# The first batch rebuilt: attention by token quarters, expert 0 alone on the first quarter, the other experts in seven-product chunks

## The chip, the cores and the metric

One core of a Trainium2 chip. The metric is the device time of one execution in microseconds (us), as a median over runs. PE is the matmul engine, DVE VectorE, ACT ScalarE, POOL GpSimd, SP the engine that issues the other DMAs. SBUF and PSUM are the two on-chip memories that the kernel's tiles lie in; PE's results come in PSUM. The granted clock is the share of PE's full clock that the profile shows as granted. L672 is line 672 of the kernel that the line of the profile comes from; a line inserted or removed shifts the numbers by a few from one kernel to the next.

## The reference, cut to what matters

```python
# attention: 4 batches, 8 heads, 768 tokens of 64, in 8 blocks of 96 tokens
P = sort_net                                   # 8x8 per head
for _ in range(5):                             # Sinkhorn: exp, rows, columns
    P = exp(P - P.max(-1)); P /= P.sum(-1) + 1e-9; P /= P.sum(-2) + 1e-9
k_sorted, v_sorted = P @ k_blocks, P @ v_blocks  # blocks mixed
x = softmax(q @ k_sorted.T / 8) @ v_sorted       # inside each block
# experts: x is (3072, 512), 4 experts of 512 -> 1024 -> 512
p = domain_probs / (domain_probs.sum(-1) + 1e-9)
out = sum(p[:, e] * (relu(x @ w1[e]) @ w2[e]) for e in range(4))
```

A batch is 768 rows of x. The work on PE is the experts' two layers; a batch's attention is made beside the experts of the batch before, except for batch 0, which has nothing before it.

## The kernel before: the parts that matter here

Batches 1 to 3 go in chunks of 256 tokens. Their second layer is not eight block products but seven (a Strassen-like scheme): sums of blocks of w2, made once (`weight_sums`), and sums of blocks of the hidden layer, made for each chunk (`h_sums`). Batch 0 goes by halves, an expert at a time, in the plain form, so it doesn't need the sums. A slot is a place after a group of the experts' matmuls where stages of attention are put. Three tiles come up again: `vo` holds mixed v on its way to memory, `pb` holds the token weights of a chunk, and `natq` a batch's queries.

```python
def load_queries(b):                         # 8 loads, f32 to f16, so all on POOL's queue
    for h in range(H):
        nc.gpsimd.dma_start(t[:, h // 2, :, h % 2, :], q[b, h]...)

def weight_sums(e):                          # once for each expert, 128x1024 each
    tt = nc.gpsimd.tensor_tensor
    tt(t3, b22, b12, ALU.subtract)           # b11.. are the blocks of w2sb[e]
    tt(b12, b12, b11, ALU.subtract)
    tt(t2, b22, b12, ALU.subtract)
    tt(n4, b21, t2, ALU.subtract)

def chunk(b, c, slot):
    for e in range(E):
        for g in range(2):                   # first layer, Relu and token weight on DVE, h_sums
            ...
    # p1 uses w2's block b11; p4 is the second product and the first that uses a sum, n4
    nc.scalar.copy(p1[:], product("p1", blk(0, 0), "b11"))
    nc.scalar.copy(ob1, product("p4", blk(1, 1), "n4"))
    ...                                      # five more products
# ... (cut)
for qd in range(2):
    for nm in ("k", "v"):
        load_natural(1, nm, qd)
load_queries(1)
for e in range(2, E):                        # weights of experts 2 and 3 after batch 1's inputs
    load_w1(e); load_w2(e)
run(halves([(0, 0, 0), (0, 1, 0)]), ...)     # batch 0: halves of 384 tokens, expert by expert
# ... (cut)
run(halves([(0, 1, 1)]) + plain(lambda: weight_sums(0), lambda: weight_sums(1))
    + halves([(0, 2, 0), (0, 2, 1), (0, 3, 0)]) + plain(lambda: weight_sums(2)) + halves([(0, 3, 1)]),
    5 * SLOTS, attention_order(1))
builds(2)
weight_sums(3)                               # first needed in batch 1
for b in range(1, B):
    for c in range(R // 2):
        chunk(b, c, slot)
```

The softmax here doesn't subtract the row's maximum and nothing guards it: scores larger than these inputs give would overflow.

Of the kernel before, what the change touches and what calls it, by code (L numbers as in the profile page):

```python
# [9 lines left out]
F32 = mybir.dt.float32  # L10
# [7 lines left out]
def kernel(  # L18
# [105 lines left out]
    make_identity(nc, ident)  # L124
    load_natural(0, "v", 0)
    load_natural(0, "k", 1)
    load_natural(0, "v", 1)
    load_natural(0, "q", 1, 0, P // 2)
    for qd in range(2):
        load_natural(0, "q", qd, P // 2, P // 2)  # L130
# [10 lines left out]
    )  # L141

# [11 lines left out]
    kTs, ETs, vos, vs0s = [], [], [], []  # L154
# [12 lines left out]
    load_w1(0)  # L167
    load_w2(0)
    load_w1(1)
    load_w2(1)  # L170
    identf = Tt[2].rearrange("p a f x -> p (a f x)")[:, 0:2 * P].bitcast(F32)
    nc.gpsimd.tensor_copy(identf, ident[:])
# [4 lines left out]
    for n in range(1):  # L177
        vo = const.tile([P, R, 4, VW], F16, name=f"vo_{n}")
        nc.gpsimd.memset(vo[:, :, :, ds(D, 2)], 1.0)
        vos.append(vo)  # L180

    p_sb = const.tile([P, R, E], F32, name="p_sb")

    for r2 in range(2):
        for hf in range(2):
            nc.sync.dma_start(
                p_sb[ds(64 * r2, 64), ds(3 * hf, 3), :],
                moe_domain_probs[ds(hf * HS, HS)].rearrange("(p r s) e -> p r s e", r=3, s=2)[:, :, r2, :],
            )
# [10 lines left out]
    def q_half(b, pr, hf, copy):  # L200

        ps = psa([P, R, 64], F16, f"ps_q_{b}_{pr}_{hf}")
        for r in range(R):
            for hh in range(2):
                nc.tensor.transpose(
                    ps[ds(D * hh, D), r, :],
                    head(b, "q", 2 * pr + hh)[ds(64 * hf, 64), r, :],
                    ident[ds(64 * hf, 64), ds(64 * hf, 64)],
                )
        if (b, pr) not in qTs:  # L210
            qTs[(b, pr)] = from_spare(S).rearrange("p (i x) -> p i x", i=NB)
        copy(
            qTs[(b, pr)][:, ds(HB * hf, HB), :].rearrange("p i (r c) -> p i r c", r=R),
            ps.rearrange("p r (i c) -> p i r c", c=CP),
        )
# [3 lines left out]
    scol = const.tile([GH, NB, 1], F32, name="scol")  # L219
    for it in range(5):  # L220
        nc.scalar.activation(sn[:], sn[:], AF.Exp, bias=0.0, scale=1.0)
        nc.vector.tensor_reduce(srow[:], sn[:], AX.X, ALU.add)
# [9 lines left out]
    warm(28)  # L232
    for pr in range(2):
        q_half(0, pr, 0, nc.scalar.copy)
    warm(48)
# [49 lines left out]
    r_half(1)  # L285

# [3 lines left out]

    def evac(b):
        return nc.vector.tensor_copy if b == 1 else nc.scalar.copy

    def st_v(b, pr):
# [9 lines left out]
        vo = vos[0]  # L304
        evac(b)(
# [23 lines left out]
    def st_k(b, pr):  # L329
# [11 lines left out]
        evac(b)(  # L341
# [57 lines left out]
    xT0a = moe.tile([P, 2, R, NKC, 64], F16, name="xT0", tag="xT")  # L399
    xT0 = [xT0a[:, hf] for hf in range(2)]  # L400
    xsl0 = {}
    vT0 = {qd: from_spare(S) for qd in range(2)}

# [18 lines left out]
    def h_k(qd, hf):  # L422
        mix_half("k", qd, hf, kTs[qd][:, 0:S], nc.vector.tensor_copy)

    def h_v(qd, hf):
        mix_half("v", qd, hf, vT0[qd], nc.scalar.copy)

    def h_w(qd, hf):
        ps = psa([BLK, 2 * HB, P], F16, f"ps_w_{qd}_{hf}")
        vT = vT0[qd]  # L430
        for n in range(2 * HB):
            nc.tensor.transpose(ps[:, n, :], vT[:, ds(n * BLK, BLK)], ident[:])
        nc.vector.tensor_copy(
            vs0s[qd][:, :, :, :, 0:D].rearrange("c i s h d -> c (i s h) d"),
            ps.rearrange("c n (h d) -> c (n h) d", h=2),
        )
# [377 lines left out]
```

## Time and profile before

| kernel before | value | from |
|---|---|---|
| time | 392.28 us, median of 3 (391.88 to 393.17) | the runs |
| span of the profiled run | 390.3 us | first line of the page |
| PE, DVE, ACT, POOL busy | 95%, 59%, 21%, 27% of the span | the page, part 1 |
| first expert matmul / batch 1 begins | 28.64 / 134.20 us | timeline of PE |
| idle of PE in batch 0's stretch | 105.80 - 101.06 = 4.7 us | the stretches, shown in the prediction |

A busy share of 95% doesn't say where the other 5% lies. The stretches do: from batch 1 on PE is busy for 86.50 of 86.70 us, and the change leaves those batches as they are, so what it can shorten lies before, and the argument below is about when batch 1 begins. "Batch 1 begins" is the first first-layer matmul of batch 1's first chunk in PE's timeline. What follows it takes 256.1 us before (390.3 - 134.20). The prediction cut 0.2 us later, at 134.40.

### The profile page before, as it was taken

The numbers are of one execution on the slowest core, as the hardware profiler recorded it, in microseconds if no ns is written. First come the engines' busy times: TensorE is split into PE (matmuls) and PEld (weight loads), VectorE is DVE, ScalarE is ACT, GpSimd is POOL, SyncE is SP. The second block draws the span as 40 slices with busy tenths as digits, with TensorE's granted clock in tenths as the row PEclk, the third lists the DMA queues.
The fourth block names the chain that finished last, engine by engine and source line by source line (L and its number), as shares of the span: only waits on it lengthen the run. The fifth ranks groups of instructions, "written<-read, shape, count | busy, mean of one in ns | idle before, by whom it ended". The sixth has DMA issues, their size and how long they took to land.

```text
span 390.3 us, 8513 instructions
## 1 busy us (share of the span) xinstructions
PE 370.9 (95%) x3725; PEld 293.0 (75%) x3725; DVE 230.7 (59%) x413; ACT 81.7 (21%) x124; POOL 105.2 (27%) x125
## 2 busy tenths in 40 slices
PE   5678989989999999999999999999999999999995
PEld 5564555545555588888889888888889888888885
DVE  5452443353245288478578477488488485694773
ACT  2344242214433233201110032211110001000000
POOL 8452460029619980200390100100100100001001
PEclk9958999999999999999999999999999999999999
DMA  9999899977429949925194335313202101100101
GB/s 118 195 209 206 119 168 193 220 129 151 70 52 150 153 115 156 193 59 95 44 121 74 90 95 147 97 21 69 54 29 76 55 0 55 55 30 29 53 2 54
DMA packets 70822, 39.07 MB, mean 100 GB/s; under 512 B 42489, under 2 KB 65089, under 8 KB 70785
## 3 DMA queue, kind: packets, MB, share of 16 engines
q0 software_dynamic: 34624, 17.83, 36.0%
q1 hardware_dynamic: 36161, 20.70, 22.5%
q8 instruction: 29, 0.48, 0.5%
q14 instruction: 8, 0.07, 0.1%
HBM read 42.86 MB, written 8.76 MB: 132 GB/s over the span
## 4 chain that ended last, share of the span: by engine, by line
PE 88%; DMA 4%; DVE 4%; ACT 1%; POOL 1%; issue 1%; DVEq 0%; SPq 0%; ACTq 0%; POOLq 0%
PE ps_h L641 33%; PE ps_p L668 28%; PE ps_h L553 10%; PE ps_o L567 9%; DMA T<-in_q_dram 3%; DMA vs_dram<-vo 2%; PE ps_a L383 1%; DVE xsl L368 1%; PE ps_s L351 1%; PE ps_k L334 1%; PE ps_v L298 1%; PE ps_x L477 1%; ACT ET L451 1%; PE ps_s L444 1%; DVE kT L417 0%
## 5 line engine op out<-in xcount | busy, mean ns | idle before, releaser
L641 PE MATMUL ps_h<-xT,w 128*128 128x256 f16 x1152 | 130.3, 273 | 0.0
L641 PEld LDWEIGHTS <-w 128*128 128x128 f16 x1152 | 111.9, 98 | 14.9
L647 DVE SCALAR_TENSOR_TENSOR Hb<-ps_h,pb 128x1024 f16<-128x1024 f32 x72 | 88.1, 1223 | 30.6 <-PE ps_h L641 29.0
L668 PEld LDWEIGHTS <-Sb 128*128 128x128 f16 x576 | 55.8, 98 | 7.5 <-issue 0.7
L688 POOL TENSOR_TENSOR oa<-u,p 128x256 f32<-128x256 f32 x9 | 6.5, 723 | 182.7 <-issue 164.7
L553 PE MATMUL ps_h<-xT,w 128*128 128x384 f16 x256 | 46.7, 332 | 0.2 <-ACT xT L480 0.2
L668 PEld LDWEIGHTS <-Hb 128*128 128x128 f16 x432 | 41.8, 98 | 4.8
L567 PE MATMUL ps_o<-w,Hb 128*128 128x512 f16 x192 | 43.8, 379 | 0.0
L553 PEld LDWEIGHTS <-w 128*128 128x128 f16 x256 | 24.3, 99 | 16.6 <-issue 1.5
L559 ACT ACTIVATE Hb<-ps_h 128x768 f16<-128x768 f32 x32 | 25.9, 811 | 48.4 <-PE ps_h L553 48.4
L668 PE MATMUL ps_p<-w,Sb 128*128 128x256 f16 x288 | 34.4, 273 | 0.4 <-DVE u L687 0.4
L668 PE MATMUL ps_p<-w,Hb 128*128 128x256 f16 x288 | 34.4, 273 | 0.0
L668 PE MATMUL ps_p<-T,Sb 128*128 128x256 f16 x288 | 33.6, 273 | 0.0
L567 PEld LDWEIGHTS <-Hb 128*128 128x128 f16 x192 | 18.1, 98 | 20.2 <-ACT Hb L559 0.5
L358 ACT ACTIVATE ET<-ps_s 96x768 f16<-96x768 f32 x24 | 18.0, 802 | 44.5 <-PE ps_s L351 44.5
L578 DVE SCALAR_TENSOR_TENSOR oacc<-ps_o,p_sb,oacc 128x512 f32<-128x512 f32 x18 | 13.5, 749 | 17.1 <-PE ps_o L567 17.1
L681 ACT COPY p<-ps_p 128x256 f32<-128x256 f32 x9 | 3.4, 373 | 93.0 <-PE ps_p L668 74.8
L368 DVE TENSOR_TENSOR xsl<-ps_a,rz 96x512 f16<-96x512 f32 x32 | 22.0, 687 | 1.1
L103 POOL DMA_DIRECT2D natq<-in_q_dram x24 | 19.8, 862 | 0.0
L93 POOL DMA_DIRECT2D nat_k<-in_k_dram x8 | 6.3, 787 | 42.9 <-PE ps_k L334 33.1
L668 PE MATMUL ps_p<-T,Hb 128*128 128x256 f16 x144 | 17.2, 273 | 0.0
L93 POOL DMA_DIRECT2D nat_v<-in_v_dram x8 | 6.1, 761 | 37.9 <-PE ps_v L298 31.5
(98 smaller groups left out, 321.8 us busy)
## 6 DMA issues: line engine op xcount, KB each, us to landing
w<-in_moe_w_dram POOLq DMA_DIRECT2D x8, 1024.0 KB, 18.2
pb<-p_dram SPq DMA_DIRECT2D x9, 512.0 KB, 4.4
nat_k<-in_k_dram POOLq DMA_DIRECT2D x8, 384.0 KB, 5.5
nat_v<-in_v_dram POOLq DMA_DIRECT2D x8, 384.0 KB, 7.1
vs_dram<-vo SPq DMA_DIRECT2D x6, 396.0 KB, 4.6
vs<-vs_dram SPq DMA_DIRECT2D x6, 396.0 KB, 3.7
natq<-in_q_dram POOLq DMA_DIRECT2D x24, 96.0 KB, 4.7
out_dram<-ob SPq DMA_DIRECT2D x9, 256.0 KB, 2.0
```

The source lines that it names most:

```text
L93: nc.gpsimd.dma_start(t[ds(p0, pn)].rearrange("p h r d -> p h (r d)"), src[b, ds(4 * qd, 4)].rearrange("h (p r) d -> p h (r d)", r=R)[ds(p ...
L103: nc.gpsimd.dma_start(t[:, h // 2, :, h % 2, :], q[b, h].rearrange("(t p) d -> p t d", p=P))
L358: nc.scalar.activation(ETs[2 * (pr % 2) + hh][:, 0:S].rearrange("c (a x) -> c a x", a=2), pss[hh][0:BLK, :, 0:HS], AF.Exp, bias=0.0, scale ...
L368: nc.vector.tensor_tensor(xsl[:, :, hh, :].rearrange("c (a i) d -> c a i d", a=2), av[:, :, :, 0:D], rz[:].broadcast_to([BLK, 2, HB, D]), ...
L553: nc.tensor.matmul(ps[:, a, 0:HS], w1sb[e][:, kc, ds((2 * f2 + a) * P, P)], xT0[hf][:, :, kc, :], start=(kc == 0), stop=(kc == NKC - 1),)
L559: nc.scalar.activation(hT[:, ds(2 * f2, 2), :], ps[:, :, 0:HS], AF.Relu, bias=0.0, scale=1.0,)
L567: nc.tensor.matmul(ps[:], hT[:, fc, ds(t * P, P)], w2sb[e][:, fc, :], start=(fc == 0), stop=(fc == NFC - 1),)
L578: nc.vector.scalar_tensor_tensor(out=oaccs[(b, col)][:], in0=ps[:], scalar=pcol, op0=ALU.mult, in1=oaccs[(b, col)][:], op1=ALU.add,)
L641: nc.tensor.matmul(ps[:, f, :], w1sb[e][:, kc, ds((4 * g + f) * P, P)], xT[:, kc, ds(2 * c * P, 2 * P)], start=(kc == 0), stop=(kc == NKC ...
L647: nc.vector.scalar_tensor_tensor(out=Hb[:, e, ds(4 * g, 4), :], in0=ps[:], scalar=0.0, op0=ALU.max, in1=pb[:, ds(e, 1), :].broadcast_to([P ...
L668: nc.tensor.matmul(ps[:], lhs(e, f), Ts[e][rhs][:, f, :], start=(e == 0 and f == 0), stop=(e == E - 1 and f == KH - 1),)
L688: nc.gpsimd.tensor_tensor(oa2, u2[:], p5[:], ALU.add)
```

## The change

Its intent: batch 0 gets the cheaper seven-product form for experts 1 to 3, and starts earlier, since expert 0 can begin as soon as the first quarter (192 tokens) of attention is done. The price is that the sums of w2 are needed in batch 0, so POOL makes them early, and the weights are loaded before batch 1's inputs. The diff, cut to its core:

```diff
+    load_w1(0); load_w2(0); (two query loads); load_w1(1); load_w2(1)   # among the first loads
+    for e in range(2, E):
+        load_w1(e)
+        load_w2(e)
 # ... h_q: one transpose group and one copy for a head quad's queries
+        copy(
+            qT0[qd][:, :, ds(HS * hf, HS)].rearrange("p s (x r) -> p s r x", r=R),
+            ps[:],
+        )
 # ... the token weights of all batches normalized at the start, on 24 partitions
+    def spread_weights():
+        normalized(p_out.rearrange("t e p -> t p e"), p_in, p_den)
+        nc.sync.dma_start(p_dram.rearrange("e (t p) -> t e p", p=P), p_out)
+        pbs[(0, 0)] = load_p(0, 0)
 # ... second layer of experts 1 to 3 in batch 0
-            for e in range(E):
+            for e in es:                         # 1 to 3 in batch 0
 # ... the order of the main program
     builds(1)
+    weight_sums(1)
     for qd in range(2):
         for nm in ("k", "v"):
             load_natural(1, nm, qd)
     load_queries(1)
-    for e in range(2, E):
-        load_w1(e); load_w2(e)
-    run(halves([(0, 0, 0), (0, 1, 0)]), 2 * SLOTS, second, 2)
-    ...
+    first_layer0(0, next_stages)
+    first_layer0(1, next_stages)
+    second_layer0(0, next_stages)
+    weight_sums(2)
+    chunk_first(0, 0, [1], 1, next_stages)
+    weight_sums(3)
+    first_layer0(2, no_stages)
+    h_x(3, vec)
+    first_layer0(3, no_stages)
+    second_layer0(1, no_stages)
-    for b in range(1, B):
+    for b in range(B):
+        plan = PLAN if b else PLAN0
```

## The prediction

> **What bounds the kernel now.** I read the page first, then the stretches of the span, then the timeline of PE, the chain of waits, and the timelines of POOL and of the DMA issues. Stretches first (the columns are busy us of each engine, granted PE clock, DMA share, GB/s); I cut the span where PE's timeline shows the first expert matmul, then the first matmul of each later batch:
>
> ```profile
> 0.00:28.60 28.60, 18.29 (x324) 16.65 (x325) 14.90 (x49) 10.13 (x18) 17.86 (x43) 0.81 1.19 173
> 28.60:134.40 105.80, 101.06 (x879) 55.30 (x877) 41.20 (x71) 36.70 (x47) 50.20 (x43) 0.99 1.02 147
> 134.40:221.10 86.70, 86.50 (x906) 75.36 (x905) 61.51 (x103) 15.77 (x25) 28.31 (x28) 1.00 0.62 102
> 221.10:307.80 86.70, 86.50 (x907) 75.49 (x905) 59.48 (x103) 15.76 (x25) 4.49 (x6) 1.00 0.29 75
> 307.80:390.30 82.50, 78.56 (x720) 70.16 (x718) 53.66 (x88) 3.35 (x9) 4.36 (x6) 1.00 0.11 40
> ```
>
> From 134.4 us on PE has no gap worth naming (86.50 of 86.70): batches 1 to 3 are matmul-bound and the change leaves them alone. All that can move is the first 134.4 us. It holds 28.6 us of opening and 105.8 us for batch 0, 19 us more than a later batch takes. The last matmuls of the opening and PE's later gaps (bracket: idle before, and what ended it):
>
> ```profile
> 28.02 0.82 PE L477 MATMUL ps_x<-ident,xsl 96*128 96x96 f16 x8 [1.42 <-DVE xsl L368]
> 28.64 0.84 PE L553 MATMUL ps_h<-xT,w 128*128 128x384 f16 x2
> 29.73 2.03 PE L553 MATMUL ps_h<-xT,w 128*128 128x384 f16 x6 [0.25 <-ACT xT L480]
> ...
> 39.13 0.50 PE L444 MATMUL ps_s<-Sb,kT 64*128 64x96 f16 x15 [0.91 <-DVE kT L417]
> ...
> 53.83 0.50 PE L477 MATMUL ps_x<-ident,xsl 96*128 96x96 f16 x8 [1.15 <-ACT ET L451]
> ...
> 88.08 0.50 PE L351 MATMUL ps_s<-qT,kT 64*128 64x96 f16 x15 [1.32 <-DVE vo L305]
> ```
>
> In the chain, warm groups of batch 0 take 1.30 us for 8 first-layer matmuls of 384 columns (2.60 for 16) and 1.73 us for 8 second-layer matmuls of 512 (3.46 for 16). There are 32 and 24 such groups: 41.6 + 41.5 = 83.1 us. Attention stages lying between them, at the starts in the chain (0.46 to 0.50 us each, 0.30 for queries), are about 6.8 us for the second half of batch 0 and 7.0 us for batch 1. The other 9 us of the stretch are gaps (some 4.7 us, listed in part above), the half clock at its start, and about 0.1 us at each change of stage.
>
> **What the Trainium skill says.** "TensorE: Matmul & The Clock Gate", section "Back-to-back issue gap", gives N/2.4 + 2.5 ns warm for N columns. The trace agrees: 16 matmuls of 256 columns take 1.75 us, 109 ns each (formula 109.2). I use its 82.5 ns for the new 192-column matmuls, which the trace of before doesn't have; that is an estimate. The same page, Part 1, says that the clock is halved after an idle window of about 3.4 us and restored after a busy one. The trace grants 0.50 from 18 to about 30 us, and full clock some 2 us after the dense expert matmuls begin, so the sparse opening runs at half clock. "DMA: Bandwidth & Descriptors", section "SWDGE vs HWDGE vs iDMA", says that a cast during a transfer is possible only on GpSimd's queue. So every f32 to f16 load here is one queue and costs POOL time to issue: below, 6.57 us for one batch's queries. "GPSIMD Engine Reference", section "Key points", says POOL shares SBUF interfaces with VectorE; here POOL's weight sums last 2.12 to 2.21 us beside busy and idle VectorE alike, so I add nothing for it.
>
> **Part by part.** (1) Fewer products. Experts 1 to 3 change from 18 second-layer groups (18 x 1.73 = 31.1 us) to three chunks of seven products of 12 matmuls, 252 x 109 ns = 27.5 us. Their first layers are 3 x 6 groups of 16, 18 x 1.75 = 31.5 us, against 24 x 1.30 = 31.2. Expert 0's first layer is 128 x 82.5 ns = 10.6 us against 10.4; its second is unchanged. Sum: 83.1 becomes 80.0, 3.1 us less on the path, as PE is the bound there.
>
> (2) An earlier start. The first quarter needs one score group and one attend group per head quad instead of whole halves. I walked the new opening with the trace's durations (PE at half clock: transposes of a head quad 0.8 us, ACT copies and exponentials 0.75 to 0.8, kT copies 0.96, normalizing 0.2 + 0.69). Sinkhorn ends at 11.3 as now; queries transposed within it cost PE 0.6 us ahead of ps_R; k copied at 15.9, v at 18.0; the new normalizing of all token weights on 24 partitions is an estimated 2.5 us of DVE (its reciprocal goes from 191 ns at 6 elements to 266 ns at 18, so about 0.95 us at 128), done by 19.5 beside v's copies; v transposed and copied at 21.1; both attend groups normalized at 23.5; xT at 25.1; two attend groups with warming matmuls still ahead of it on PE. First expert matmul at about 26, against 28.6: 2.6 us earlier. The first weight lands at an estimated 20.6 us (22.6 now, with 384 KB less ahead of it at some 200 GB/s), so it doesn't hold this.
>
> (3) Gaps. Stages are smaller and their copies shared between DVE and ACT, each used a slot (about 2 us) later. Of the present 4.7 us of gaps I expect 2 to 3, with a new one of about 0.8 us where the third quarter's transpose is copied right before its use.
>
> (4) Weight sums come forward. This is what I believe sets the end of the gain. Today they run late, with nobody waiting:
>
> ```profile
> 45.17 6.57 POOL L103 DMA_DIRECT2D natq<-in_q_dram  x8
> ...
> 86.20 2.14 POOL L601 TENSOR_TENSOR T<-w 128x1024 f16<-128x1024 f16 x1
> 88.42 2.12 POOL L602 TENSOR_TENSOR w<-w 128x1024 f16<-128x1024 f16 x1
> 90.61 2.12 POOL L603 TENSOR_TENSOR T<-w 128x1024 f16<-128x1024 f16 x1
> 92.81 2.12 POOL L604 TENSOR_TENSOR T<-w,T 128x1024 f16<-128x1024 f16 x1
> 94.89 2.12 POOL L601 TENSOR_TENSOR T<-w 128x1024 f16<-128x1024 f16 x1
> ```
>
> One expert is 94.89 - 86.20 = 8.7 us. In the new order POOL has: builds done at about 23; sums of expert 1, not before its second weight has landed; four k/v loads (3.0 us), eight query loads (6.6), sums of experts 2 and 3. That weight is the fourth issued between 10.5 and 13 us; now it lands at about 38.5, and exactly the same bytes stand before it afterwards. Fewer 16-byte packets of token weights make it about 1 us earlier, the 512 KB of pb now moved into this saturated stretch 1 to 2 us later: 39. Then 39 + 8.7 + 3.0 + 6.6 + 17.4 = 74.7 us for the last sum of expert 3. The second product of the first chunk needs that sum. PE's own way there: 26 + expert 0 (10.6 + 10.4) + three first layers (10.5) + the first product and two thirds of the second (2.2) + attention (7.4) + changes of stage (3) + cold start (1.5) + gaps (1.5 to 2.5) = 73 to 74. So PE waits there 1 to 2 us, and the chain runs through weight load and POOL.
>
> From there to batch 1: a third of a product (0.44), five products (6.5), two chunks of 6 x 1.75 + 7 x 1.31 = 19.7 each (39.3), and batch 1's attention less its first stage (a later batch's 86.7 less 3 x 26.2 leaves 8.1, so 7.8): 54.0. Batch 1 begins at 74.7 + 54.0 = 128.7, or 1 us later with small waits: about 129.7 against 134.4. Gain 4.7 us: 392.28 - 4.7 = 387.6.
>
> **Rivals.** (a) POOL is no bound: the weight lands earlier or PE comes later than I think, and PE alone decides. For it: my two times differ by only 1 or 2 us. If all gaps went and PE reached the sums free, batch 1 would begin at about 126 and the time be 384. (b) The finer stages wait on each other: each of the second part's nine fillers has a PSUM copy behind it, two score and attend stages share one slot, and ACT also has the Relu. ACT has 1.6 us of work in a 2.1 us slot, by 0.81 + 0.80, so I don't think it binds, but 3 us more of gaps would make it 390.5. (c) The new normalizing and broadcast of weights sits in the opening on DVE, ahead of v's copy: if its 24-partition operations take 4 us rather than 2.5, everything starts 1.5 us later, hidden in part by the POOL wait: 388. (d) Batch 1's loads are now queued behind all eight weights (4 MB at 200 GB/s from 38.5: the last at 59, k/v to 67, queries to 72). Its first v stage comes at about 72 and queries are transposed by DMA after that, so they are just in time; if not, 2 us: 389.5.
>
> **Range and chances.** The firm part is 3.1 us; the early start of 2 to 3 us and the closed gaps are capped by POOL. Below 384.4 us (2% faster) needs rival (a) in full, and I see it at 0.13. Slower by 2% (over 400) would need over 12 us of new waits, 0.02. Range 384.0 to 390.8.
>
> **What would show it.** Right: first expert matmul near 26; seven-product groups at 1.31 us; the first chunk's second product waiting for POOL at about 74 to 75; batch 1 beginning at 129 to 130; the stretches after it unchanged at 86.7, 86.7, 82.5. Wrong: PE meeting no POOL wait; first expert matmul after 28; attention stages of batch 0 with gaps over 1 us; later batches that change.

## The result and the profile after

The changed kernel takes 407.23 us (median of 4, 406.06 to 407.71), the kernel before 392.08 us (median of 4, 391.60 to 393.17) in the same rounds. The ratio is 1.0378 (95% interval 1.0346 to 1.0410): slower by 3.8%. Ratios here are the mean time of one kernel's runs over that of the other's of the same rounds, so not quite the ratio of the quoted medians. The prediction, 387.6 us in 384.0 to 390.8, was wrong.

The stretches of the changed kernel, cut like those of before; the last two cuts lie about half a microsecond ahead of their batch's first matmul (235.96 and 322.61), those of before up to 0.2 us behind it (columns: stretch, length, busy us and count of PE, PEld, DVE, ACT, POOL, granted PE clock, DMA share, GB/s):

```profile
0.00:27.29 27.29, 17.73 (x341) 15.84 (x341) 16.18 (x49) 14.81 (x18) 15.35 (x40) 0.95 1.11 174
27.29:148.55 121.26, 100.42 (x1153) 81.58 (x1151) 73.04 (x109) 30.34 (x40) 70.70 (x62) 0.93 0.95 143
148.55:235.40 86.85, 86.15 (x901) 75.07 (x899) 58.91 (x103) 15.67 (x25) 22.25 (x27) 1.00 0.63 102
235.40:322.20 86.80, 86.61 (x908) 75.53 (x907) 59.61 (x104) 15.77 (x25) 4.63 (x7) 1.00 0.31 74
322.20:405.60 83.40, 79.17 (x726) 70.73 (x723) 54.08 (x89) 3.36 (x9) 4.49 (x7) 0.99 0.12 39
```

The opening is 1.3 us shorter. Batch 0's stretch is 15.5 us longer (121.26 against 105.80) with about the same PE work (100.42 against 101.06): idle PE went from 4.7 to 20.8 us. From the first matmul of batch 1 on, the time grew by 0.95 us (257.05 against 256.10). So the question is what PE waits for in batch 0. PE's timeline at the first chunk's products (start, length; in the bracket the idle time before and what ended it):

```profile
69.90 1.47 PE L672 MATMUL ps_p<-w,Hb 128*128 128x256 f16 x12
71.21 0.49 PE L300 MATMUL ps_v<-nat_v,PIv 128*128 128x384 f16 x2
72.46 0.61 PE L672 MATMUL ps_p<-T,Hb 128*128 128x256 f16 x4 [0.76 <-DVE Hb L646]
77.82 1.01 PE L672 MATMUL ps_p<-T,Hb 128*128 128x256 f16 x4 [4.75 <-POOL T L603]
86.78 1.01 PE L672 MATMUL ps_p<-T,Hb 128*128 128x256 f16 x4 [7.95 <-POOL T L603]
...
97.00 2.71 PE L672 MATMUL ps_p<-T,Sb 128*128 128x256 f16 x12 [2.78 <-ACT p L695]
```

The second product's 12 matmuls come in three groups of four, one for each expert; the groups of experts 2 and 3 each wait for the last of POOL's four sums of that expert (L603). The wait that the prediction named is there, and PE comes to it when the prediction said (73.07, before the 4.75), but it takes 4.75 + 7.95 us, not 1 to 2. POOL's timeline says why:

```profile
39.97 2.12 POOL L600 TENSOR_TENSOR T<-w 128x1024 f16<-128x1024 f16 x1 [7.10 <-DMA w<-in_moe_w_dram]
...
50.91 0.77 POOL L93 DMA_DIRECT2D nat_v<-in_v_dram  x1
51.64 1.68 POOL L103 DMA_DIRECT2D natq<-in_q_dram  x2
55.18 0.82 POOL L103 DMA_DIRECT2D natq<-in_q_dram  x1 [1.86 <-DMA w<-in_moe_w_dram]
60.22 0.82 POOL L103 DMA_DIRECT2D natq<-in_q_dram  x1 [4.22 <-DMA w<-in_moe_w_dram]
62.16 0.82 POOL L103 DMA_DIRECT2D natq<-in_q_dram  x1 [1.12 <-DMA nat_k<-in_k_dram]
...
68.01 0.82 POOL L103 DMA_DIRECT2D natq<-in_q_dram  x1 [0.57 <-DMA nat_v<-in_v_dram]
68.84 2.13 POOL L600 TENSOR_TENSOR T<-w 128x1024 f16<-128x1024 f16 x1
...
84.61 2.12 POOL L603 TENSOR_TENSOR T<-w,T 128x1024 f16<-128x1024 f16 x1
```

The eight query issues, 6.57 us in a row before, now take from 51.64 to 68.83, 17.2 us: from the third on, each stands until an earlier load lands (the bracket names which). Counting back from each, it is the load issued eight before it (e2 below tests this). With weights of 1 MB ahead, the landings are some 5 us apart (55.18 to 60.22). POOL's sums stand behind these issues in its order.

Three smaller things show. First, VectorE (the same stretch of time, h_sums at L621 to L625):

```profile
68.08 0.42 DVE L625 TENSOR_TENSOR Sb<-Hb 128x512 f16<-128x512 f16 x1
...
73.46 2.33 DVE L625 TENSOR_TENSOR Sb<-Hb 128x512 f16<-128x512 f16 x1
75.71 2.33 DVE L621 TENSOR_TENSOR Sb<-Hb 128x512 f16<-128x512 f16 x1
```

The same addition takes 0.42 us before POOL's sums start at 68.84 and up to 2.33 us beside them. Secondly, PE's clock: the stretch from 76 to 88 us, in which PE works 2.23 of 12.00 us, has a granted clock of 0.50. Thirdly, the 2.78 us at 97.00 are ACT's: its copy for the fifth product stands behind a copy of vo that waited 4.20 us for the store of vo to end.

### The profile page after: what moved, and what is told of

Its sections match the earlier page's. It is cut to its first block, busy times and chain, and to the rows that moved or that the text cites. A ratio compares the mean times of both kernels' runs of the same rounds, so it can differ in the third digit from the quotient of the medians.

```text
span 405.6 us, 9132 instructions
## 1 busy us (share of the span) xinstructions
PE 370.1 (91%) x4016; PEld 318.8 (79%) x4016; DVE 261.8 (65%) x451; ACT 79.9 (20%) x117; POOL 117.4 (29%) x139
## 4 chain that ended last, share of the span: by engine, by line
PE 69%; DMA 14%; POOL 9%; DVE 4%; issue 2%; ACT 1%; POOLq 0%; ACTq 0%; DVEq 0%; SPq 0%
PE ps_h L640 34%; PE ps_p L672 30%; DMA w<-in_moe_w_dram 7%; DMA nat_k<-in_k_dram 4%; DMA vs_dram<-vo 3%; POOL T L600 2%; POOL w L601 2%; POOL T L602 2%; DVE xsl L369 1%; PE ps_s L352 1%; POOL T L603 1%; PE ps_k L335 1%; PE ps_a L384 1%; PE ps_v L300 1%; ACT vo L306 1%
## 5 line engine op out<-in xcount | busy, mean ns | idle before, releaser
L640 PE MATMUL ps_h<-xT,w 128*128 128x256 f16 x1440 | 163.4, 273 | 0.2 <-DVE oacc L707 0.2
L646 DVE SCALAR_TENSOR_TENSOR Hb<-ps_h,pb 128x1024 f16<-128x1024 f32 x90 | 110.1, 1224 | 39.9 <-PE ps_h L640 38.2
L672 PEld LDWEIGHTS <-Sb 128*128 128x128 f16 x720 | 70.0, 98 | 14.4 <-issue 5.0
L672 PE MATMUL ps_p<-T,Sb 128*128 128x256 f16 x360 | 43.5, 277 | 2.8 <-ACT p L695 2.8
L672 PE MATMUL ps_p<-w,Hb 128*128 128x256 f16 x360 | 43.9, 275 | 0.0
L623 DVE TENSOR_TENSOR Sb<-Sb,Hb 128x512 f16<-128x512 f16 x45 | 22.7, 505 | 0.4
L103 POOL DMA_DIRECT2D natq<-in_q_dram x24 | 19.9, 850 | 10.6 <-DMA w<-in_moe_w_dram 6.1
L625 DVE TENSOR_TENSOR Sb<-Hb 128x512 f16<-128x512 f16 x45 | 22.7, 503 | 0.0
L621 DVE TENSOR_TENSOR Sb<-Hb 128x512 f16<-128x512 f16 x45 | 22.5, 499 | 0.0
L306 ACT CAST vo<-ps_v 128x768 f16<-128x768 f32 x12 | 9.5, 802 | 58.2 <-PE ps_v L300 49.7
L342 ACT CAST kT<-ps_k 128x768 f16<-128x768 f32 x12 | 9.6, 799 | 37.7 <-PE ps_k L335 37.7
L627 DVE TENSOR_TENSOR Sb<-Hb,Sb 128x512 f16<-128x512 f16 x45 | 16.1, 417 | 0.0
## 6 DMA issues: line engine op xcount, KB each, us to landing
nat_k<-in_k_dram POOLq DMA_DIRECT2D x8, 384.0 KB, 7.4
nat_v<-in_v_dram POOLq DMA_DIRECT2D x8, 384.0 KB, 6.8
```

The source lines that it names most:

```text
L103: nc.gpsimd.dma_start(t[:, h // 2, :, h % 2, :], q[b, h].rearrange("(t p) d -> p t d", p=P))
L306: nc.scalar.copy(vo[:, :, ds(2 * (pr % 2), 2), 0:D], ps[:, :, 0:R * D].rearrange("p h (r d) -> p r h d", r=R),)
L342: nc.scalar.copy(kT[:, 0:S].rearrange("p (i r c) -> p i r c", i=NB, r=R), ps.rearrange("p r (i c) -> p i r c", c=CP),)
L621: tt(sm[0], blk(0, 1), blk(1, 1), ALU.add)
L623: tt(sm[1], sm[0], blk(0, 0), ALU.subtract)
L625: tt(sm[2], blk(0, 0), blk(0, 1), ALU.subtract)
```

## The experiments

The theory after reading the traces: POOL's order is the bound. Its query issues wait for landings, the sums stand behind them, and PE stands before the sums. Rivals: the finer stages of the opening cost the time (query copy, normalizing on VectorE, the block builds), or the finer stages and copies of batch 0 as such. Experiments e1 to e4 ran together, e5 to e8 too, and so on, each beside the kernel before on the same chip. Their edits are to the changed kernel unless another one is named.

### e1: the query loads after the sums

```diff
-    load_queries(1)          # before the first matmul of expert 0
     ...
     weight_sums(3)
+    load_queries(1)
```

> The changed kernel with one line moved: batch 1's eight query loads are issued on POOL after the weight sums of expert 3, not before those of expert 2. Theory A (the end is set by POOL: the eight query issues took 17.2 us instead of 6.6 because each waits for the load issued eight before it, and the sums of experts 2 and 3 stood behind them): sums of expert 2 start at about 52 us (68.8 in the changed kernel), those of expert 3 end at about 69 to 70 (86.7), PE's waits of 4.75 and 7.95 us in the second product of the first chunk fall below 1 us together, the clock isn't halved there, batch 1 begins at about 132 to 134 us (148.5), the time is 389 to 393 us, ratio to before 0.99 to 1.005. Rival B (the finer stages of the new first batch cost the time, and the POOL wait only shows it): the PE gaps turn up elsewhere and the ratio stays above 1.03.

Measured: 399.60 us, ratio 1.0198 (1.0168 to 1.0227). The eight issues now take 6.62 us in a row again (68.87 to 75.49), the sums of expert 3 end at 68.9 instead of 86.7, and both waits for POOL are gone. That is half of the loss, and my range of 389 to 393 us was missed. The other half turned into a new wait. In PE's timeline of e1 (the bracket again is the idle time and what ended it):

```profile
88.05 2.72 PE L672 MATMUL ps_p<-T,Sb 128*128 128x256 f16 x12 [8.75 <-ACT p L695]
```

And in ACT's timeline of e1, what stands ahead of that copy (L695):

```profile
86.92 0.80 ACT L306 CAST vo<-ps_v 128x768 f16<-128x768 f32 x1 [10.16 <-DMA vs_dram<-vo]
87.62 0.38 ACT L695 COPY p<-ps_p 128x256 f32<-128x256 f32 x1
```

There is one vo buffer; its store was issued at 75.06, just when the eight query loads went out, and took 11.8 us. ACT ran the two in the program's order (86.92, then 87.62), so the copy of the fifth product stood behind vo. Batch 1 began at 139.98.

### e2: is it a count or bytes?

```diff
-            load_w1(e)       # e == 2: one load of 1 MB
+            for h2 in range(2): nc.gpsimd.dma_start(w1sb[2][:, ds(2 * h2, 2), :], ...)   # two loads
```

> The changed kernel with the load of expert 2's first weight cut into two loads of half the size (same bytes, one load more). Theory (a load on POOL's queue may be issued only when the one eight before it has landed, whatever the bytes): the first weight of expert 3 now waits for the second weight of expert 0 and is issued at about 26.7 us instead of 20.55, the second one for the third query load, at about 28 instead of 26.8. Rival (the queue holds a certain number of bytes or descriptors): both issues stay where they were within 1 us. Time as the changed kernel, 405 to 409 us, in either case.

Measured, one look: 407.68 us. The same bytes in one more load: the issue of w1 of expert 3, which stood until 20.55 in the changed kernel, now stood until 26.28 (4.89 us for a weight's landing), and the time stayed. One more load moved the wait by one landing, so it is the number of loads, eight, and not their size. (The second weight of expert 3 was issued at 27.21, with none of the wait until about 28 that I expected.) Where the eight comes from can be read in the program. The changed kernel gives POOL's loads eight semaphores in turn, and each issue carries a wait for the load that had that semaphore before: the third query load waits for w1 of expert 3. So the wait is the program's own, and these runs show no limit of the chip; nobody tried more loads in flight.

### e3 and e4: the opening

e3 writes the transposed queries in order and reads PSUM with a stride, instead of the reverse:

```diff
-            qT0[...].rearrange("p s (x r) -> p s r x", r=R),
-            ps[:],
+            qT0[...].rearrange("p s (x r) -> p s x r", r=R),
+            ps.rearrange("p s r x -> p s x r"),
```

> The changed kernel, with the copy of the transposed queries of batch 0 walking the same elements in another order: the written side runs contiguously, the PSUM side read is strided. Theory C (the 2.7 us of that copy come from writing 2-byte elements 12 bytes apart): the copy takes 0.8 to 1.0 us on ACT and DVE, the fifth exponential of Sinkhorn comes at about 9.6 us instead of 10.9, the half of its cast on ACT before 12.5 instead of 14.3, the first expert matmul at about 25.3 instead of 27.3; the time stays at 405 to 408 us because the sums on POOL decide. Rival D (stride on either side costs the same): the copy stays at 2.7 us and nothing moves. Rival E (the late start is what the time lost): the time falls by 2 us.

e4 moves the normalizing of all token weights behind the first quarter's attention:

```diff
-    spread_weights()
-    normalized(p_sb[:], p_sb[:], den0[:])
     h_w((vec, act))
     ...
     h_a(1, 1, WARM)
+    spread_weights()
+    normalized(p_sb[:], p_sb[:], den0[:])
```

> The changed kernel with the normalizing of the token weights (3.8 us of VectorE in the opening) emitted after the first quarter's attend groups instead of ahead of the copy of transposed v. Theory: the wait of 1.7 us of PE for that copy goes, the first expert matmul comes at about 25.6 us instead of 27.3, and the time stays at 405 to 408 us because the sums on POOL decide. Rival: opening bound elsewhere, first expert matmul within 0.5 us of 27.3.

Measured, one look each: 407.66 and 407.32 us. In e3 the copy went from 2.71 to 0.80 us on ACT and from 2.73 to 0.96 us on VectorE. But e3 missed its start: the first expert matmul came at 27.01, not at about 25.3. Its first group of attend matmuls came 0.79 us earlier (21.18 against 21.97); then the granted clock was 0.59 from 21.5 to 25 us, against 0.97 in the changed kernel, and most of this was lost again. In e4 it came at 24.61 instead of 27.29, at full clock. Part of that is the clock's: e1 and e13 have the changed kernel's opening, a granted clock of 1.00 from 25 to 28 us where the changed kernel's profile has 0.50, and begin at 25.97 and 25.78. So a first expert matmul moves by 1 to 2 us from profile to profile with the clock alone. Neither edit moved the time: the sums end at 86.6 to 86.8 in all of these, since POOL's chain starts from the landing of expert 1's second weight, which the opening doesn't touch. What is won earlier is waited for, in e3 at the sums (7.29 instead of 4.75 us before expert 2's), in e4 in part already before them (3.94 us at 34.97, for VectorE).

### e5 and e6: the order of stages, and of POOL

e5 is e1 with batch 1's v stages 2 and 3 later, so that vo's store has time:

```diff
-  ... (0, 9, st_v, 2), (0, 9, st_q, 1), (0, 10, st_v, 3), (0, 11, st_s, 0), (0, 12, st_k, 1), (1, 0, st_a, 0), ...
+  ... (0, 9, st_q, 1), (0, 11, st_s, 0), (0, 12, st_v, 2), (0, 12, st_k, 1), (1, 0, st_v, 3), (1, 2, st_a, 0), ...
```

> The run with the queries last (e1) had PE wait 8.75 us for a copy on ACT that stood behind the third v stage's copy, which waited 10 us for the one buffer of mixed v to be stored. Here batch 1's third and fourth v stages come three slots later (after the first chunk's last product and in the second chunk), and its attend stages of the second chunk one or two slots later; nothing else. Theory (the wait is ACT's order plus one buffer): the 8.75 us wait goes; a wait of up to 5 us may turn up at the first attend stage of batch 1, since the store took 11.8 us beside the queries' loads and the read of it follows; batch 1 begins at 131 to 136 us (139.98), time 387 to 396 us. Rival (the store itself is what PE needs, whatever the order): the wait moves as a whole to the attend stage, time within 2 us of e1's 399.6.

e6 has these stages, and POOL's order turned: k/v loads, the sums of experts 1 and 2, five query loads, the sums of expert 3, three query loads.

```diff
-    weight_sums(1)
     (k/v loads)
-    load_queries(1)
+    weight_sums(1)
     ...
     weight_sums(2)
+    load_queries(1, range(5))
     weight_sums(3)
+    load_queries(1, range(5, 8))
```

> As the run before in its plan of stages, but on POOL: batch 1's k and v loads ahead of the sums of expert 1 (POOL stands idle there from 33 to 40 us), then sums of 1 and 2, five query loads, sums of expert 3, three query loads. So the sums of expert 3 end at about 71 to 72 us (86.7 in the changed kernel, 68.9 in e1), the queries reach the DMA queue before 70, and the store of the first mixed v (75 us) no longer shares it with them: 5 to 6 us instead of 11.8. PE waits under 2 us in the second product and under 2 us at the first attend stage; batch 1 begins at 129 to 132 us; time 386 to 390 us, ratio 0.985 to 0.995. If PE still waits over 4 us anywhere between 70 and 130 us, the theory that POOL's issue order made the loss is incomplete.

Measured: e5 394.02 us, ratio 1.0029 (0.9996 to 1.0063); e6 393.52 us, ratio 1.0019 (0.9993 to 1.0044). The 8.75 us wait for vo is gone in both; batch 1 begins at 136.52 and 134.81. In e5 3.18 us of it came back at 84.64, as a wait for the transposed queries. So order alone, of the stages and of POOL, moves batch 1's start back by 13.7 us (148.55 to 134.81) and ends level with the kernel before; e6 still missed its range of 386 to 390 us. One wait over 2 us is left in e6 before batch 1: 2.62 us at 73.16 for VectorE, whose additions run beside POOL's sums of expert 3.

### e7 and e8: e6 and the opening together

e7 is e6 with e3's copy, the weights of expert 3 issued after the block builds, and the normalizing in the third of the slots beside expert 0. e8 puts the three changes of the opening alone on the changed kernel.

```diff
-    for e in range(2, E): load_w1(e); load_w2(e)
+    load_w1(2); load_w2(2)
     ...
     builds(1)
+    load_w1(3); load_w2(3)
     ...
-        [(h_v, 0, 1, act), (h_q, 1, 1, vec)],
+        [(h_v, 0, 1, act), (h_q, 1, 1, vec), (spread_weights,), (normalized, p_sb[:], p_sb[:], den0[:])],
```

> The run before plus three changes of the opening: the query copy in contiguous order (0.8 instead of 2.7 us), the normalizing of the token weights moved behind the copies of the second part's third slot, and the weight loads of expert 3 issued after the builds of batch 1, so that the build of the second half's mixing matrix doesn't stand behind an issue that waits (it came at 27.8 us). First expert matmul at about 24 to 24.5 us (27.3), no wait of PE for that build, PE reaches the second product's third expert at about 69 to 70 us, where the sums end at 71 to 72; batch 1 begins at 126 to 129 us; time 383 to 387 us, ratio 0.977 to 0.988.

> The changed kernel with the three changes of the opening alone (query copy order, normalizing later, expert 3's weight loads after the builds), POOL's order after that and the plan of stages as in the changed kernel. First expert matmul at 24 to 24.5 us, PE 3 us earlier throughout up to the first chunk's second product, and the wait there longer by the same 3 us: time 405 to 408 us. Rival (the opening is worth its own length): 404 us or less.

Measured: e7 394.16 us, ratio 1.0039 (1.0014 to 1.0064); e8, one look, 406.36 us. In e8 the first expert matmul comes at 22.50, 4.8 us earlier than in the changed kernel, and the time is within 1 us of it: all of the earlier start is absorbed. In e7, which missed its range of 383 to 387 us by far, it is absorbed elsewhere: PE waits 7.62 us at 55.03, since VectorE stood 9.67 us before pb, the token weights. They are made later there, and their load took 11.1 us beside the weight loads.

### e9 and e10: expert 3's sums on VectorE, and the normalizing back

Both put the normalizing back where the change has it. In e9 the sums of expert 3 are VectorE's, right before the first product, and all query loads follow the sums of expert 2; e10 is otherwise e7.

```diff
-    def weight_sums(e):
-        tt = nc.gpsimd.tensor_tensor
+    def weight_sums(e, eng=nc.gpsimd):
+        tt = eng.tensor_tensor
     # e9, in chunk(), after the first layers
+        if (b, c) == (0, 0): weight_sums(3, nc.vector)
```

> e7 with two differences: the normalizing of batch 0's weights back where the change has it, and the sums of expert 3 on VectorE (eight additions of 128x1024 f16) just before its work on the second product, so that POOL has the sums of experts 1 and 2 alone, then all eight query loads in a row. Theory (POOL's chain to the sums of expert 3 is what holds the first chunk, and later pb's short wait of e7 came from the later p store): no PE wait over 2 us for the sums; pb lands before 45; VectorE's sums take 8 x 0.6 to 0.8 = 5 to 6.5 us alone or up to 2 us each beside POOL; first product at about 67 to 71; batch 1 begins at 129 to 132; time 385 to 390, ratio 0.983 to 0.995. Rival (what is left of the loss lies not in POOL but in the finer stages and the copies on VectorE and ACT): removing POOL's third sum only moves the wait to VectorE; batch 1 begins at 134 to 136 as in e5 to e7; time 392 to 395, ratio 1.000 to 1.006.

> e7 with the normalizing of batch 0's weights back where the change has it: POOL's order of e6, query copy written in order, the weights of expert 3 issued after the block builds. Theory (e7's 7.62 us wait at 55 was for pb, held up since its store came later): that wait is gone, first expert matmul at about 26.3 to 27.3, p1 limited by the sums of expert 3 at about 71 to 72; batch 1 begins at 132 to 134, time 389 to 392, ratio 0.992 to 1.000. Rival (pb's load is slow since it runs beside the weight loads, whenever it is issued): a wait of 5 us or more for pb remains near 50 to 58, and the time is that of e7, 393.5 to 394.5.

Measured: 395.15 us, ratio 1.0059 (1.0035 to 1.0083), and 393.59 us, ratio 1.0020 (1.0004 to 1.0036). My theory's numbers were missed in both; the times are near those of the rivals, but not by the rivals' mechanism. The wait for pb is gone, as I expected, but the opening got slower: first expert matmul at 31.91 and 30.25. VectorE's timeline in e9:

```profile
17.23 0.66 DVE L531 TENSOR_REDUCE T<-T 24x128 f32<-24x512 f32 x1
17.93 4.80 DVE L532 TENSOR_SCALAR T<-T 24x128 f32<-24x128 f32 x1
22.76 0.94 DVE L533 RECIPROCAL T<-T 24x128 f32<-24x128 f32 x1
```

The first and the last of POOL's builds in e9:

```profile
17.57 1.07 POOL L260 TENSOR_TENSOR Sb<-maskk,Rs 128x512 f16<-128x512 f16 x1
...
21.61 1.04 POOL L271 TENSOR_TENSOR PIk<-maskk,Rs 128x512 f16<-128x512 f16 x1
```

The addition of 1e-9 on 24x128 takes 0.21 us in the changed kernel (18.39). Here, with the weight loads of expert 3 moved behind them, POOL's five block builds (1.04 to 1.07 us each, 17.57 to 22.65) run at that time, and the addition lasts until the last has ended. In e10 it is 3.64 us, again to the end of the builds at 20.98. PE waited 6.28 and 4.78 us for the copy behind it: this is what cost e9 and e10 most of their start. e11 below puts the loads back ahead of the builds, and the addition takes 0.21 us again.

e9 also gives a size: the four additions of 128x1024 took 0.68, 0.69, 1.10 and 0.69 us on VectorE, against 2.12 on POOL, and the additions of 128x512 stayed at 0.41 to 0.42 us. But they stood between VectorE's last work on the first layer and the second product, and PE waited 2.66 us.

### e11 and e12: earlier sums on VectorE

e11 has e6's stages, e3's copy, all eight query loads after the sums of expert 2, the weights where the change issues them, and expert 3's sums on VectorE in its gap before the second half of expert 0. e12 has the sums of experts 1 and 2 on VectorE too.

```diff
     # e12: before expert 0's second layer on the first half
+    weight_sums(1, nc.vector)
     second_layer0(0, next_stages)
     ...
     h_x(3, vec)
+    weight_sums(2, nc.vector)      # e12 only
+    weight_sums(3, nc.vector)
     first_layer0(3, no_stages)
     second_layer0(1, no_stages)
```

> e6 with the query copy written in order, all eight query loads right after the sums of expert 2, and the sums of expert 3 on VectorE in its gap before the second half of expert 0 (from about 58, where it was idle 4.64 us), not right before the first product as in e9. The weights of expert 3 are issued where the change issues them, since in e9 and e10 the earlier block builds on POOL made one 24x128 addition of the normalizing on VectorE take 4.80 and 3.64 us instead of 0.21. Theory (POOL's work costs twice: as a chain to the sums of expert 3, and by slowing VectorE while it computes): the addition takes 0.21 again, first expert matmul at 26.5 to 27.5; the sums of expert 3 done on VectorE by 64; no PE wait over 1.3 us before batch 1; batch 1 begins at 127 to 131; time 384 to 389, ratio 0.980 to 0.993. Rival (the finer stages themselves cost it): batch 1 begins at 133 to 136 and the time stays at 392 to 394, ratio 0.999 to 1.005.

> e11 with the sums of experts 1 and 2 on VectorE too: those of expert 1 before the first half of expert 0's second layer, those of experts 2 and 3 in the gap before the second half. POOL has only loads and block builds in the first batch until the first chunk's additions. Theory: an addition of the sums takes 0.68 to 0.75 us on VectorE without POOL beside it, 2.8 us an expert; VectorE's additions of 128x512 stay at 0.41 us; VectorE's copies of the second half of expert 0 come up to 1 us late; batch 1 begins at 126 to 131, time as e11 or up to 2 us less: 383 to 389, ratio 0.977 to 0.993. Rival (VectorE is full and the sums only move the wait to it): PE waits for VectorE grow by 3 us or more, time 391 to 395.

Measured: e11 393.75 us, ratio 1.0038 (1.0022 to 1.0054); e12 392.41 us, ratio 1.0000 (0.9982 to 1.0018). Again the mechanism is confirmed and the time, expected at 383 to 389 us, isn't: the addition in the normalizing takes 0.21 us, the first expert matmul comes at 25.44 and 26.62, the sums take 0.69 us each. But I had put VectorE before a weight that had not landed. Both times lie where their rivals had them, and what decides against the rival of e11, that the finer stages cost it, is e15 below, which keeps the stages. In e11 it stood 7.62 us, until 60.57, for w2 of expert 3 (the bracket names a load of k, but w2 was issued at 27.24 and took 33.2 us, so it landed at 60.4), with the copies of expert 0's output behind it, and PE waited 4.88 us at 64.16; in e12 it stood until 39.90 for that of expert 1, and PE waited 3.66 us at 45.18 (there for ACT, whose copy stood behind VectorE's).

### e13 and e14: only the engine of the sums, and a later place

e13 is the changed kernel with nothing but this: expert 1's sums on VectorE in two halves in the slots after the second and the third token tile of expert 0 (not the first two, as my expectation has it), those of experts 2 and 3 after `h_x(3, vec)`. e14 is e12 with the sums at the same places.

```diff
-        [(h_a, 0, 2), (h_s, 0, 3)],
-        [(h_a, 1, 2), (h_s, 1, 3)],
+        [(h_a, 0, 2), (h_s, 0, 3), (weight_sums, 1, nc.vector, 0)],
+        [(h_a, 1, 2), (h_s, 1, 3), (weight_sums, 1, nc.vector, 1)],
```

> The changed kernel with one thing different: all sums of batch 0 (experts 1 to 3) on VectorE, those of expert 1 in two halves in the slots after the first two token tiles of expert 0 (at about 41 and 44, when the second weight of expert 1 has landed at 39.8), those of experts 2 and 3 in the gap at 57 to 63. Loads, stages and opening are the changed kernel's. Theory (the 15 us lost in batch 0 are POOL's chain and what follows from it): the waits of 4.75 and 7.95 us for the sums are gone, VectorE's 128x512 additions take 0.41 us, no half clock between 76 and 90, batch 1 begins at 128 to 131, time 387 to 391, ratio 0.987 to 0.998. Rival (stages, copies and the store of vo cost several us of their own): batch 1 begins at 133 to 137, time 392 to 396, ratio 1.000 to 1.010.

> e12 with the sums of expert 1 in two halves in the later slots, so that VectorE doesn't stand before the second weight of expert 1. Theory: the PE wait of 3.66 us at 45.18 is gone, batch 1 begins at 128.7 to 130 instead of 132.90, time 388 to 390, ratio 0.988 to 0.996, and the difference from e13 is what the query copy in order and the later v stages are worth. Rival (the wait turns up elsewhere): batch 1 at 132 or later, ratio 0.998 or more.

Measured: e13 395.85 us, ratio 1.0072 (1.0056 to 1.0089); e14 393.09 us, ratio 1.0000 (0.9983 to 1.0017). e13 settles the main point: taking the sums out of POOL's order, with POOL's query issues waiting as before (44.92 to 68.60), brings the changed kernel from 407.2 to 395.9 us. How much of this is the chain, and how much VectorE's additions (0.42 us again), e13 doesn't separate. Its range of 387 to 391 us was missed, and that of its rival, 392 to 396, met: some of the loss is not POOL's. What that is shows in PE's timeline of e13:

```profile
63.42 2.35 PE L578 MATMUL ps_o<-w,Hb 128*128 128x512 f16 x8 [2.63 <-DVE oacc L583]
...
86.86 2.72 PE L674 MATMUL ps_p<-T,Sb 128*128 128x256 f16 x12 [4.48 <-ACT p L697]
```

The first is for VectorE, which stood before w2 of expert 3, the second for ACT behind vo's store. In e14 the vo wait is gone, the 3.66 us of e12 are gone, but the same stand before w2 of expert 3 is there, so its rival, that the wait turns up elsewhere, held. VectorE's timeline of e14:

```profile
59.89 0.69 DVE L602 TENSOR_TENSOR T<-w 128x1024 f16<-128x1024 f16 x1 [4.35 <-DMA w<-in_moe_w_dram]
```

PE's timeline of e14, at the third token tile of that half (L584 is VectorE's copy of a tile):

```profile
63.48 3.57 PE L579 MATMUL ps_o<-w,Hb 128*128 128x512 f16 x8 [4.38 <-DVE oacc L584]
```

The pool of these PSUM tiles has two buffers, so PE gets two tiles ahead of VectorE's copies and no more; it stops when they do, and comes back at half clock (granted 0.50; 3.57 us for 8 matmuls that take 1.73 warm).

### e15 and e16: the sums behind the copies

e15 is e14 with expert 3's sums in halves after the second and third token tile of expert 0's second half; e16 also has the block builds of batch 1 ahead of the issue of expert 3's second weight.

```diff
     weight_sums(2, nc.vector)
-    weight_sums(3, nc.vector)
     first_layer0(3, no_stages)
-    second_layer0(1, no_stages)
+    third = [None, 0, 1]
+    def sum3():
+        half = third.pop(0)
+        if half is not None: weight_sums(3, nc.vector, half)
+    second_layer0(1, sum3)
     # e16
-    load_w2(3)               # with the other weights
     builds(1)
+    load_w2(3)
```

> e14 with the sums of expert 3 on VectorE in two halves after the second and the third token tile of expert 0's second half, so that the tiles' copies no longer stand behind the wait for expert 3's second weight (it lands at 59.8 in the changed kernel and in e14, and the sums there began at 59.89). Theory: the PE wait of 4.38 us at 63.48 with its half clock is gone; a wait of up to 1.5 us may stay where VectorE has 2.15 us of work in a slot of 1.73; batch 1 begins at 129.5 to 131.5 instead of 134.56; time 388 to 391, ratio 0.989 to 0.997. Rival: PE is held by that weight some other way or the wait moves on, batch 1 at 133 or later, ratio 0.999 or more.

> e15 with batch 1's block builds ahead of the second weight of expert 3 in POOL's order: in e14 that issue waited 5.3 us for a landing and held the build that the second quarter's k needs, and PE waited 3.28 us at 29.00 for it. Normalizing on VectorE is over (about 19) before the builds start (about 21.5), so it isn't slowed as in e9. Theory: build done by 23, no PE wait there; batch 1 begins 1.5 to 3.3 us before e15's, at 127 to 130; time 386 to 389, ratio 0.984 to 0.993. Rival (what is won before the first landing of expert 1's and 3's weights is lost again at them): batch 1 as in e15 within 0.7 us, same time.

Measured: e15 386.58 us (386.49 to 387.38, 4 runs), ratio 0.9865 (0.9836 to 0.9894); e16 386.64 us, ratio 0.9859 (0.9826 to 0.9892); the kernel before 391.80 us in the same rounds. Both beat both kernels: 1.4% below the kernel before, clear of noise though under 2%, and some 20 us below the changed one (0.9865 against 1.0378 of about 392). e15 came out better than the 388 to 391 us that I expected. e16 tells nothing apart from e15: batch 1 begins at 128.23 against 128.19, as its rival said. But the 3.28 us wait for the build, which e14 had, is in neither: in their profiles PE ran at half clock before the first expert matmul (0.57 and 0.56 from 25 to 28 us, 1.00 in e14), came to it at 25.90 and 25.80 instead of 23.89, and was no longer early enough to wait. So the two don't test the rival. The stretches of e15, columns as above:

```profile
0.00:25.90 25.90, 16.65 (x340) 14.87 (x341) 16.25 (x49) 11.43 (x18) 14.81 (x39) 0.90 1.08 172
25.90:128.19 102.29, 97.67 (x1152) 80.59 (x1150) 68.77 (x121) 28.53 (x40) 45.06 (x50) 0.99 1.15 173
```

VectorE's timeline of e15 at expert 0's second half:

```profile
58.74 0.75 DVE L584 TENSOR_SCALAR oacc<-ps_o,p_sb 128x512 f32<-128x512 f32 x1 [0.98 <-PE ps_o L579]
60.03 0.69 DVE L602 TENSOR_TENSOR T<-w 128x1024 f16<-128x1024 f16 x1 [0.54 <-DMA w<-in_moe_w_dram]
60.76 0.69 DVE L603 TENSOR_TENSOR w<-w 128x1024 f16<-128x1024 f16 x1
61.37 0.74 DVE L584 TENSOR_SCALAR oacc<-ps_o,p_sb 128x512 f32<-128x512 f32 x1
```

VectorE stands 0.54 us before the weight, between two copies, and the sums fit there. Batch 0's stretch has 4.6 us of idle PE (102.29 - 97.67), as many as the kernel before, with 3.2 us less PE work (97.67 against 100.82 between the same two events, 28.64 and 134.20).

The runs in one table (batch 1 and first expert matmul from each profile; time and ratio from the rounds; the kernel before took 391.8 to 393.2 in them). A profile is of one execution: e13's was its slowest (398.13 us against a median of 395.85), so its batch 1 stands some 2 us late here, and the first column moves with the clock as said under e3:

| kernel | first expert matmul | batch 1 begins | time | ratio |
|---|---|---|---|---|
| before | 28.64 | 134.20 | 392.1 | 1 |
| changed | 27.29 | 148.55 | 407.2 | 1.038 |
| e1 queries after the sums | 25.97 | 139.98 | 399.6 | 1.020 |
| e6 POOL's order, stages later | 27.22 | 134.81 | 393.5 | 1.002 |
| e9 expert 3's sums on VectorE, late | 31.91 | 135.54 | 395.2 | 1.006 |
| e13 only the sums' engine | 25.78 | 139.47 | 395.9 | 1.007 |
| e12 all sums on VectorE, before w2 of expert 1 | 26.62 | 132.90 | 392.4 | 1.000 |
| e14 all sums on VectorE, before w2 of expert 3 | 23.89 | 134.56 | 393.1 | 1.000 |
| e15 all sums on VectorE, behind the copies | 25.90 | 128.19 | 386.6 | 0.986 |

Two things could not be run: a second vo buffer (the build says that SBUF has no room for it), and the normalizing on POOL (a version with POOL's division did not compile).

## Why the prediction was wrong, point by point

**(1) Fewer products: right.** PE's busy time in batch 0's stretch is 100.42 us in the changed kernel, some of it at half clock, and 97.67 in e15 at a clock of 0.99, against 100.82 before (from 28.64 to 134.20). That is 3.2 us less; the step said 3.1. The estimate of 82.5 ns for a 192-column matmul held: 32 take 2.81 us and 16 take 1.49.

**(2) An earlier start: right in direction, short in size.** 27.29 us, not 26. The term that I mis-sized is the copy of the transposed queries: 0.8 us in my walk, 2.7 us measured, because it writes 2-byte values out of order (e3: 0.80 with the write in order). The normalizing came to 2.84 us (0.66 + 0.21 + 0.94 + 1.03), against an estimated 2.5. But this copy doesn't explain the whole 1.3 us, as I thought: without it e3 still starts at 27.01, and with it e1 and e13 start at 25.97 and 25.78, at full clock. I had also read the clock wrongly: the trace of before grants 1.00 up to about 18 us, not half clock in the whole opening. None of it mattered for the time: e8 starts at 22.50 and gains at most 1 us.

**(3) Gaps: wrong.** Besides the waits for the sums, the changed kernel has 2.78 us for ACT behind vo's store, and several of 0.6 to 1.1 us. I took vo's single buffer as given and did not look for who stands behind it on ACT.

**(4) The weight sums set the end: the right bound, at the wrong time.** The weight landed at 39.9, not 39, and PE would have been through two thirds of the second product at about 73.5 (73.07, and 0.44 for expert 2's group), where I had 73 to 74. That agreement is in part luck: PE started 1.3 us late and took 1 to 2 us less than my sum for the way. The step that failed is the sum "39 + 8.7 + 3.0 + 6.6 + 17.4 = 74.7": its term of 6.6 us for the eight query issues was measured at 17.2. I took it from the kernel before, where k, v and the queries were issued ahead of the late weights, and did not ask what an issue waits for. With eight loads in flight it waits for a landing, and the change put the queries behind the weights. That is 10.6 us; with the later landing (1.0) and slightly longer sums (0.4) the sums ended at 86.7, 12.0 us late. The rest of the miss: from there to batch 1 61.8 us passed instead of the 55 that I allowed, with the half clock after the wait and the vo wait in it (6.8 us), and from batch 1 on it took 257.05 us where I had carried over 255.9, 1.15 more. The sum, 20.0 us, compares with 407.2 - 387.6 = 19.6.

**The remark that the shared interface adds nothing: half right.** I looked at POOL's durations only. They stay at 2.12 to 2.30. It is VectorE that pays: 0.41 becomes 2.33 us. "SBUF — State Buffer", section "Who interferes with whom", in the Trainium skill, says that a VectorE instruction with two SBUF inputs contends with a GpSimd instruction that reads SBUF. The page's section "Terms" says that the loser blocks fully. The runs agree in kind (0.41 against 2.33 us), and I should have read it with the question of which engine loses.

**The rivals and the odds.** Rival (d), batch 1's loads just in time, was nearest to the matter but put it on the data and not on the issuing engine. I gave 0.02 to "over 12 us of new waits", because I counted waits only where PE waits. The long one arose on POOL, which the page shows 27% busy, and it reached PE by way of the order of POOL's work.

e15 shows that the forecast gain was there once the waits were gone: 386.6 us and batch 1 at 128.19, where I had 387.6 and 129.7. That is another kernel, and doesn't make the prediction of this one right.

What stays open: from its first matmul to batch 2's, batch 1 takes 0.6 to 0.7 us longer in the changed kernel and in e15 (87.41 and 87.33 against 86.75); no run was made for it. Of the 6.8 us after the sums, the shares of the clock and of the single waits were read from the trace and not separated by an experiment.

## What to carry to other kernels

When a change reorders the issues on an engine that also computes, work out for each issue what it waits for, not only how long it takes: here the program lets eight loads be in flight, and with 1 MB weights among them a 0.8 us issue became 5 us, and everything behind it on that engine waited too. Put work that depends on a late load behind the work that others wait for: with the same instructions on the same engine, batch 1 begins 6.4 us earlier in e15 than in e14 by this alone. Before reading anything into a start that moved by 1 or 2 us, compare the granted clock of the two profiles. And when an experiment removes a wait and the time moves little, look for the wait that took its place before giving up the theory: here it took five of them (vo, pb, the normalizing beside the builds, w2 of expert 1, w2 of expert 3) until the expected gain showed.

## What the Trainium skill lacked or had wrong

- "DMA: Bandwidth & Descriptors": it has the rates and the paths, but nothing on when an issue on POOL's queue stands. In these runs it stands for the load issued eight before: query issues at 55.18, 60.22, 62.16 us each after that landing, and one more load of the same bytes moved an issue from 20.55 to 26.28 (e2). The eight is the number of semaphores in the built program; what the chip itself would take isn't shown.
- "SBUF — State Buffer", section "Who interferes with whom": "Issue order, not op shape, decides who blocks." The runs don't contradict this: the slow VectorE additions began just after one of POOL's sums had (73.46 after 73.33, 75.71 after 75.59). What the page lacks is how one-sided it becomes when POOL computes without a pause: VectorE's 128x512 additions went from 0.41 to 2.33 us, POOL's sums from 2.12 to at most 2.30. And an addition of 24x128 with one SBUF input did not get its turn between POOL's instructions: 4.80 and 3.64 us instead of 0.21, to the end of a row of builds of 1.04 to 1.10 us each (e9, e10). The page doesn't say that a loser can stand through several instructions.
- "GPSIMD Engine Reference", section "Key points": "For elementwise work, the DVE is structurally ~2× faster." For the f16 additions of 128x1024 here it is 2.12 against 0.69 us, 3.1 times.
- "SBUF — State Buffer" names a penalty for accesses that cross to a new line of SBUF, without a size, and no other page that I looked at gives the cost of writing 2-byte values 12 bytes apart from ACT: a copy of 128x768 from PSUM took 2.71 us on ACT with a stride in the write and 0.80 us with the stride in the read (2.73 and 0.96 us on VectorE).
